# Attention, a 2-D Fourier mix and a split-precision feed-forward on one core: zero products at the start, the second weight's preparation moved later, scale passes tied to finished heads, and a new table of planned times

## The chip, the cores and the metric

The kernel runs on one core of a Trainium2 chip. The metric is the device time of one execution in microseconds (us). The profiled execution is one more run of the same program, recorded by the hardware profiler.

Engines are named as in the profile: PE is TensorE (PEld its weight loads), DVE is VectorE, ACT is ScalarE, POOL is GpSimd, SP is SyncE, whose queue issues nearly all the transfers. Each engine works its own instructions off in order.

## The reference, cut to what matters

```python
# batch B=8, heads H=8, sequence S=576, head size D=64, model width 512, hidden width 2048
scores = q @ k.T / sqrt(D) + slopes[h] * (-abs(i - j))      # only 0 <= i-j < 128, else -1e9
attn   = exp(scores - max); attn /= attn.sum(-1) + 1e-9
x      = (attn @ v)  ->  (B, S, 512)
u      = x + real(fft(fft(x, axis=1), axis=2))
un     = (u - mean(u)) / sqrt(var(u) + 1e-6)
out    = u + relu(un @ w_ch1) @ w_ch2
```

## The kernel before

**Work of a batch.** A batch has four pairs of heads. A pair has scores on PE (`scores`), an exponential with its bias and row minimum on DVE and ACT, a transposition of the probabilities, and products with v (`values`); `weigh` (DVE) divides a finished head into the batch's tile X. After four pairs `fourier` transforms X: `fold_a` to `fold_d` on DVE and ACT, `rows`, `middle` and `cols` as products on PE, evictions on ACT and DVE, sums back into X. `norm` normalizes the rows (DVE, POOL, ACT) and a transposing transfer writes the tile uT. Last comes `ffn`: per tile of 256 rows it has 16 steps of up-products (12 matmuls of 256 columns a step, two steps to a bank) and then, for each 128 rows, 48 down-products of 512 columns. An eviction of hidden values is one ACT instruction (`ACTIVATE hbuf<-fp`, 144 in all) and one of DVE. The up- and down-products share two banks of PSUM (pool `ps_f`).

**Two kinds of pairs.** Batches 0 and 1 (`b < NF`) compute scores and values in 32-bit and transpose on PE (`turn`). Batches 2 to 7 split every operand into two 16-bit parts, and their probabilities are transposed by transfers on SP's queue (`flip`). To split they need a scale of q, k and v of the whole batch. `batch_scales` makes it in a pass: `fetch` brings a 128 by 512 piece of the batch's data into a slot (there are two slots), `part` squares and sums it on ACT, fifteen pieces a batch, six batches, so ninety parts; then `top` and `scale`.

**Weights.** Each of the two weights comes as 64-bit words in sixteen pieces of 512 KB. A piece is loaded, `rebias` (ACT) and `join` (DVE, two instructions) make 32-bit numbers of it, and `gram` (PE, four products) measures it. From the sum of the grams comes a scale, and `high` (ACT) and `low` (DVE) split the weight into two 16-bit planes. `wall_109` holds the first weight, `wall_110` the second.

**Products without use.** After every turn of batches 0 and 1, `warm` multiplies 184 columns into a part of the `pv` bank that nobody reads: `SPIN` times in batch 0, `SPIN1` times in batch 1.

**The order.** Each function is put into a queue with a planned time (`put(t, f)`), and the times come from a table of constants. A scheduler of the framework then sets the order of each engine's instructions from its own estimate of durations, so that an instruction with a later planned time can stand earlier where its inputs are there.

Of the kernel before, what the change touches and what calls it, by code (L numbers as in the profile page):

```python
# [22 lines left out]
NF = 2  # L23
# [17 lines left out]
TGRP = ((0, 1), (2, 3), (4,))  # L41


LB, LC = 2, 5
DFT = 29.33
START = 49.19
PACE, T1 = (0.442, 0.509), 11.5
SPIN, GAP = 6, 1.03
SLOW = 1.318
W2A, W2D, W2B, W2E = 4.44, 0.778, 21.6, 0.559  # L50
W1D, W1B, W1E = 0.507, 13.0, 0.6
F0 = 6.38
SW=184
SPIN1 = 3


def begin_of(p):
# [20 lines left out]
def attn_fft_ffn_kernel(  # L78
# [39 lines left out]
    A.dma_start(out=tab1_sb, in_=tab1)  # L118
    A.dma_start(out=tab2_sb, in_=tab2)
    A.activation(misc[:, 12:13], half[:, 0:1], AF.Exp)  # L120
    stack = const.tile([128, 512], F16, name="stack")
    stack1 = const.tile([128, 1], F16, name="stack1")
    G.memset(stack, 0.0)
    G.memset(stack1, 0.0)
    vhs = const.tile([128, 2, 2, 5, 65], F16, name="vhs")
    G.memset(vhs[:, :, :, :, 64:65].rearrange("p a b c d -> p (a b c) d"), 1.0)
# [2 lines left out]
                    for o in range(0, 4096, 512)])  # L129

    wall = [const.tile([128, 9, 1024], F32, name=f"wall{i}") for i in range(2)]
    mslots = cycle([wall[0][:, 8, o:o + 512] for o in (0, 512)])
    wf = [t.bitcast(F16).rearrange("p s (e x) -> p s e x", e=2) for t in wall]

    def w1_ap(e, c, f):
# [30 lines left out]
    stage = xp.tile([128, 5, DM], F32, name="X").rearrange("p a b -> p (a b)")  # L166

    ready = set()

    def weights(wi, t0, dt, t1, dt1):  # L170
        w, top = ((w1, 2.0 ** 7), (w2, 2.0 ** 14))[wi]
# [54 lines left out]

        for c in range(16):
            t = t0 + dt * c
            put(-3 + 0.1 * c if c < ns else t + dt * (1 - ns) - 0.05, load, c)
            put(t, rebias, c)  # L230
            put(t + dt - 0.1, join, c)
            put(t + 2 * dt - 0.3, gram, c)
# [17 lines left out]
    def batch_scales(b, t0, dt):  # L250
        box = {}

        def begin():
            box["mx"] = small.tile([128, 3, 5], F32, name="mx", tag="mx")
            G.memset(box["mx"], 0.0)

        def fetch(x, fl, o, n):
            assert (0, 7) in ready
            box[x] = next(mslots)[:, 0:n]
            nc.sync.dma_start(out=box[x], in_=fl[:, o:o + n])  # L260

        def part(x, i, c):
            t = box.pop(x)
            A.activation(t, t, AF.Square, accum_out=box["mx"][:, i, c:c + 1])  # L264

        def top():
            m1 = small.tile([128, 3], F32, name="m1")
            V.tensor_reduce(m1, box["mx"], AX.X, ALU.max)
            box["sums"] = total(m1)

        def scale():
            r = small.tile([128, 3], F32, name="r")
            root_inv(r, box["sums"])
            sc = small.tile([128, 8], F32, name="sc", bufs=3)
            V.tensor_scalar_mul(sc[:, 0:1], r[:, 0:1], 2.0 ** -58)
# [12 lines left out]
        put(t0 - 2.5 * dt, begin)  # L288
        x = 0
        for i, (src, n) in enumerate(((q, NQ * 4), (k, NK * 4), (v, 2560))):  # L290
            fl = src[b].rearrange(("j p s -> (j p s)", "h p c d -> (h p c d)")[i == 2])
            fl = fl.rearrange("(p x) -> p x", p=128)
            for c, o in enumerate(range(0, n, 512)):
                put(t0 + dt * (x - 1.8), fetch, x, fl, o, min(512, n - o))
                put(t0 + dt * x, part, x, i, c)
                x += 1
        put(t0 + dt * x, top)
        put(t0 + dt * x + 0.6, scale)

# [37 lines left out]
    def convert(p, what):  # L337
# [8 lines left out]
        if what < 2:  # L346
            pair = att.tile([128, 2, NQ], F16, name="qk"[what] * 2)
            n, s = ((NQ, nsl[:, 8 + j:9 + j]), (NK, sc[:, 1:2]))[what]
            hi, lo, src = pair[:, 0, 0:n], pair[:, 1, 0:n], raws[p][what]
            ops.setdefault(p, []).extend((hi, lo))  # L350
        else:
            s = sc[:, 2:3]
            vh = vhs[:, p % 2]
            vl = att.tile([128, 2, 5, D], F16, name="vl")
            hi = vh[:, :, :, 0:D].rearrange("p a b c -> p (a b) c")
            lo = vl.rearrange("p a b c -> p (a b) c")
            src = raws.pop(p)[2].rearrange("p a b c -> p (a b) c")
            ops[p] += vh, vl
# [100 lines left out]
    def weigh(p, e, pv):  # L459
        b, j = divmod(p, 4)  # L460
        h = 2 * j + e
        if h == 0:
            Xs[b] = xp.tile([128, 5, DM], F32, name="X")
        ri = small.tile([128, 5], F32, name="ri")
# [287 lines left out]
    for p in range(4 * B):  # L752
        b, j = divmod(p, 4)
        t, f = begin_of(p), 1 if b else PACE[0]
        lead = t - 7 * f if p else -3.2
        if p == 4:
            lead = max(lead, begin_of(3) - 3.7 * PACE[0])
        put(lead, load, p)
        if b < NF:
            put(t - 3.8 * f if p else -2, convert, p, 0)  # L760
            put(t - 1.2 * f, load_v, p)
            put(t + 4.2 * f, v_max, p)
        else:
            early = p < 4 * NF + 2
# [9 lines left out]
        if b < NF and j == 3:  # L774
            put(t + 5 * f, f32_scale, b)

    def step(g, t, dt):
        if next(g, g) is not g:
            put(t + dt, step, g, t + dt, dt)

    for b in range(B):
        t = begin_of(4 * b)
        if b >= NF:
            batch_scales(b, *((t - 16.4, 0.72) if b == NF else (t - 26, 1.2)))
        fourier(b, transform_of(b))
# [121 lines left out]
```

## Time and profile before

| | us |
|---|---|
| median of 3 runs (lowest to highest) | 1096.65 (1095.37 to 1097.96) |
| profiled execution | 1097.29 |
| its span, first to last instruction | 1095.5 |
| PE busy | 1047.4 |
| DVE busy | 700.9 |
| ACT busy | 586.0 |

The time of the profiled execution is 1.8 us longer than its span. "Busy" counts modelled ends of pipelined matmuls, so that a busy PE is not one at its peak. A granted clock of 1.00 is 2.4 GHz, of 0.50 is 1.2 GHz.

### The profile page before, as it was taken

To read this page: it belongs to the slowest core of one execution; us is meant where nothing else is said; L and a number is where in the kernel's file an instruction comes from. 1 tells how busy PE (TensorE), PEld (TensorE's weight loads), DVE (VectorE), ACT (ScalarE), POOL (GpSimd) and SP (SyncE) were. 2 spreads that over 40 slices of the span, in tenths; PEclk is the share of its full clock that TensorE was granted. 3 is DMA by queue.
4 is the path that set the end of the run, shared out by engine and by line. 5 is a ranking of instruction groups with operands and counts; after the bars stand their busy time and mean duration, and the time that the engine had idled before them with its cause. 6 is when DMAs were issued, how large, how long until landed. Compare 5 with 4: busy or idle time off the path is not lost.

```text
span 1095.5 us, 23888 instructions
## 1 busy us (share of the span) xinstructions
PE 1047.4 (96%) x9254; PEld 734.7 (67%) x9254; DVE 700.9 (64%) x2073; ACT 586.0 (53%) x1388; POOL 23.8 (2%) x61
## 2 busy tenths in 40 slices
PE   6999989988897999999999999999899999999998
PEld 4886776574655677676757578585758576757655
DVE  4889588558783775959685857777776726252111
ACT  6887888667755674557534745466545512241000
POOL 0000000001000000001000000001000000000000
PEclk9997869999999999999999999999999999999999
DMA  9961475656676364424722454326412410020000
GB/s 370 347 202 55 121 182 160 187 147 145 140 192 182 77 137 88 99 64 73 163 69 69 101 100 87 95 50 124 118 46 46 89 33 10 11 58 11 20 11 20
DMA packets 191506, 117.81 MB, mean 108 GB/s; under 512 B 154400, under 2 KB 164128, under 8 KB 191392
## 3 DMA queue, kind: packets, MB, share of 16 engines
q1 hardware_dynamic: 190816, 114.84, 41.5%
q8 instruction: 72, 1.18, 0.5%
q10 hardware_dynamic: 576, 1.45, 0.3%
q14 instruction: 42, 0.34, 0.1%
HBM read 70.63 MB, written 9.44 MB: 73 GB/s over the span
## 4 chain that ended last, share of the span: by engine, by line
PE 68%; DMA 11%; DVE 8%; ACT 8%; issue 3%; SPq 1%; ACTq 0%; DVEq 0%
PE fp L728 27%; PE fp L743 25%; PE sp L384 5%; PE pv L448 3%; DMA wall<-k_dram 2%; PE pd L579 2%; ACT wall L264 2%; DMA wall<-v_dram 2%; DMA wall<-q_dram 2%; ACT P L163 2%; PE pv L305 1%; DMA pt<-P 1%; DVE P L396 1%; PE pd L613 1%; DMA kr<-k_dram 1%
## 5 line engine op out<-in xcount | busy, mean ns | idle before, releaser
L743 PE MATMUL fp<-wall,hbuf 128*128 128x512 f16 x1728 | 391.2, 380 | 1.9 <-DVE hbuf L163 1.8
L728 PEld LDWEIGHTS <-wall 128*128 128x128 f16 x3840 | 338.1, 98 | 62.9 <-issue 20.0
L728 PE MATMUL fp<-uT,wall 128*128 128x256 f16 x3072 | 365.7, 275 | 14.3 <-DVE hbuf L163 8.5
L743 PEld LDWEIGHTS <-hbuf 128*128 128x128 f16 x1728 | 164.1, 98 | 190.8 <-issue 6.4
L163 ACT ACTIVATE P<-P,nb 128x256 f32<-128x256 f32 x320 | 142.8, 478 | 98.8 <-DVE nb L396 98.3
L733 ACT ACTIVATE hbuf<-fp 128x512 f16<-128x512 f32 x144 | 85.1, 592 | 194.5 <-PE fp L728 194.4
L163 DVE SCALAR_TENSOR_TENSOR hbuf<-fp,hbuf 128x512 f16<-128x512 f32 x144 | 98.3, 683 | 97.5 <-ACT hbuf L733 97.3
L396 DVE CUSTOM_DVE_ANT_0 P<-sp,rg,nsl 128x256 f32<-128x256 f32 x240 | 98.3, 450 | 46.1 <-PE sp L384 38.6
L163 DVE SCALAR_TENSOR_TENSOR P<-P 128x256 f16<-128x256 f32 x240 | 89.0, 391 | 30.5 <-ACT P L409 29.5
L384 PE MATMUL sp<-kk,qq 64*128 64x256 f16 (+4 forms) x880 | 96.1, 296 | 8.3 <-DMA kk<-k_dram 5.5
L409 ACT ACTIVATE P<-P 128x256 f16<-128x256 f32 x240 | 85.3, 383 | 6.6 <-DMA pt<-P 6.1
L264 ACT ACTIVATE wall<-wall 128x512 f32<-128x512 f32 (+2 forms) x90 | 54.5, 606 | 49.5 <-DMA wall<-v_dram 18.4
L453 PE MATMUL pv<-vhs,pt 128*128 128x65 f16 x432 | 54.8, 195 | 4.8 <-DMA pt<-P 3.8
L163 DVE SCALAR_TENSOR_TENSOR X<-fp,misc,X 128x512 f32<-128x512 f32 x32 | 23.9, 746 | 54.1 <-PE fp L743 54.1
L454 PE MATMUL pv<-vl,pt 128*128 128x64 f16 x432 | 54.7, 193 | 0.0
L455 PE MATMUL pv<-vhs,pt 128*128 128x65 f16 x432 | 54.6, 194 | 0.0
L453 PEld LDWEIGHTS <-pt 128*128 128x128 f16 x432 | 40.9, 98 | 14.1 <-DMA pt<-P 4.8
L384 PEld LDWEIGHTS <-qq 64*128 64x128 f16 (+1 forms) x720 | 31.8, 100 | 24.4 <-issue 20.2
L448 PE MATMUL pv<-vr,pt 128*128 128x65 f32 x288 | 46.7, 307 | 0.4 <-issue 0.3
L448 PEld LDWEIGHTS pv<-vr,pt 128*128 128x128 f32 x288 | 43.2, 225 | 3.6 <-issue 1.8
L728 PE MATMUL fp<-wall,wall 128*128 128x128 f16 x768 | 45.0, 219 | 0.0
L454 PEld LDWEIGHTS <-pt 128*128 128x128 f16 x432 | 40.6, 99 | 5.9
(156 smaller groups left out, 1177.5 us busy)
## 6 DMA issues: line engine op xcount, KB each, us to landing
qr<-q_dram SPq DMA_DIRECT2D x32, 304.0 KB, 3.1
hbuf<-w_dram SPq DMA_DIRECT2D x16, 512.0 KB, 7.6
out_dram<-X SPq DMA_DIRECT2D x32, 256.0 KB, 2.4
wall<-v_dram SPq DMA_DIRECT2D x30, 256.0 KB, 2.8
vr<-v_dram SPq DMA_DIRECT2D x24, 320.0 KB, 3.3
kr<-k_dram SPq DMA_DIRECT2D x24, 289.0 KB, 3.3
wall<-q_dram SPq DMA_DIRECT2D x24, 256.0 KB, 2.9
wall<-k_dram SPq DMA_DIRECT2D x24, 256.0 KB, 2.9
```

The source lines that it names most:

```text
L163: put(now[0] + dt, lambda: f(*a, **kw))
L264: A.activation(t, t, AF.Square, accum_out=box["mx"][:, i, c:c + 1])
L384: T.matmul(sp[e][:m, col:col + n], qq[h, c0:c0 + m], keys(kk[h], ti), start=(x == 0), stop=(x == len(prods) - 1))
L396: V.tensor_tensor_reduce(pt[:m, 0:n], sp[e][:m, col:col + n], tab[:m, pc:pc + n], mul, 3.0e38, ALU.add, ALU.min, nb[:m, ti:ti + 1])
L409: A.activation(hi, P32, AF.Copy, scale=2.0 ** 14)
L448: T.matmul(pv[:, ti], pt[:, col:col + 128], ops[p][2][:, e, vc], start=first, stop=last)
L453: T.matmul(pv[:, ti], ph, vh[:, e, vc], start=first, stop=False)
L454: T.matmul(pv[:, ti, 0:D], ph, vl[:, e, vc], start=False, stop=False)
L455: T.matmul(pv[:, ti], pl, vh[:, e, vc], start=False, stop=last)
L728: T.matmul(fp[:, i * n:(i + 1) * n], w1_ap(e, c, f0 + i), uT[:, j, c, 0:n], start=(c == 0 and p == 0), stop=(c == 3 and p == 2))
L733: A.activation(ht[:, 0], fp, AF.Relu)
L743: T.matmul(op, hh[f][:, a, i * 128:(i + 1) * 128], w2_ap(e, f), start=(f == 0 and p == 0), stop=(f == 15 and p == 2))
```

## The change

- **Products from the start.** Twenty matmuls of 512 zero columns (`stack`, now the first tile that POOL fills after `ident`) stand ahead of the first scores and write the bank `pv`; with the bank there, `warm` runs after batch 0's first turn too.
- **Fewer products later.** `SPIN` goes from 6 to 5 and `SPIN1` from 3 to 1. Counted in the order of PE, there are 138 such matmuls in batch 0 before and 120 now, and 72 in batch 1 before and 24 now.
- **Second weight.** Its planned start `W2A` goes from 4.44 to 13.895, its first loads come behind those of the first weight (`WL`).
- **Scale passes.** For batches 3 to 7 a one-element copy on POOL reads the head that `weigh` finished last by plan and writes the slot, and the transfer into the slot waits for the copy: 75 copies. These batches have three slots instead of two.
- **The table.** All planned times are new; `E0` adds a delay once, after the sixteenth step of the feed-forward.

```diff
-LB, LC = 2, 5
-SPIN, GAP = 6, 1.03
-W2A, W2D, W2B, W2E = 4.44, 0.778, 21.6, 0.559
-SPIN1 = 3
+LB, LC = 2, 5.046
+E0 = 18.423
+W1A, N0 = 1.058, 20
+SPIN, GAP = 5, 0.73
+W2A, W2D, W2B, W2E = 13.895, 0.631, 21.285, 0.429
+SPIN1 = 1
...
-    mslots = cycle([wall[0][:, 8, o:o + 512] for o in (0, 512)])
+    mslots = [wall[0][:, 8, 0:512], wall[0][:, 8, 512:1024], wall[1][:, 8, 512:1024]]
+    turns, held = count(), set()
...
-            put(-3 + 0.1 * c if c < ns else t + dt * (1 - ns) - 0.05, load, c)
+            put(WL[wi] + 0.1 * c if c < ns else t + dt * (1 - ns) - 0.05, load, c)
...
         def fetch(x, fl, o, n):
             assert (0, 7) in ready
-            box[x] = next(mslots)[:, 0:n]
-            nc.sync.dma_start(out=box[x], in_=fl[:, o:o + n])
+            slot = next(turns) % (3 if (1, 7) in ready and b > NF else 2)
+            assert slot not in held
+            held.add(slot)
+            box[x] = slot, mslots[slot][:, 0:n]
+            if b > NF:
+                G.tensor_copy(box[x][1][0:1, 0:1], last[-1])
+            nc.sync.dma_start(out=box[x][1], in_=fl[:, o:o + n])
...
-                put(t0 + dt * (x - 1.8), fetch, x, fl, o, min(512, n - o))
+                put(t0 + dt * (x - (FL if b > NF else min(FL, 1.95))), fetch, x, fl, o, min(512, n - o))
...
+    pv = ps_v.tile([128, 512], F32, name="pv")
+    spare_cols["pv"] = pv[:, 512 - SW:512]
+    for _ in range(N0):
+        T.matmul(pv, stack[:, 0:128], stack, start=True, stop=True)
...
+        last.append(Xs[b][0:1, 0, h * D:h * D + 1])
...
     def step(g, t, dt):
         if next(g, g) is not g:
-            put(t + dt, step, g, t + dt, dt)
+            steps[0] += 1
+            t += dt + (E0 if steps[0] == 16 else 0.0)
+            put(t, step, g, t, dt)
```

**ACT during batch 1's transform.** Before, between the evictions of the row products (`zh`, L583) and the first of the middle ones (`gt`, L601), parts of the scale passes (L264, on `wall_109`) stand among them:

```order
L264 ACTIVATE wall_109,mx<-wall_109 128x512 x2
L733 ACTIVATE hbuf<-fp 128x512
L583 ACTIVATE zh_2810<-pd 128x289
L733 ACTIVATE hbuf<-fp 128x512
L359 ACTIVATE vhs<-vr,sc 128x10x64
L264 ACTIVATE wall_109,mx<-wall_109 128x512
L264 ACTIVATE wall_109,mx<-wall_109 128x384
L583 ACTIVATE zh_2847<-pd 128x289
L733 ACTIVATE hbuf<-fp 128x512
L264 ACTIVATE wall_109,mx<-wall_109 128x512 x2
L601 ACTIVATE gt<-pd,sc 128x1 x2
```

Now the same place (`zh` is L606, `gt` L624, evictions of hidden values L757) has none:

```order
L606 ACTIVATE zh_2672<-pd 128x289
L428 ACTIVATE P<-P 96x256
L757 ACTIVATE hbuf<-fp 128x512
L624 ACTIVATE gt<-pd,sc 128x1 x2
L624 ACTIVATE gt<-pd,sc 33x1
L625 ACTIVATE gt<-gt 128x1 x2
L625 ACTIVATE gt<-gt 33x1
L757 ACTIVATE hbuf<-fp 128x512
L644 ACTIVATE ab<-pd,gt,sc 128x65
```

Counted over ACT's whole order, the parts that stand ahead of the 1st, 8th, 16th, 36th, 72nd and 90th of the 144 evictions of hidden values were 19, 27, 56, 90, 90 and 90 before, and are 14, 18, 30, 45, 75 and 90 now.

**PE at the start.** Before, PE begins with the first pair's scores (L384):

```order
L384 MATMUL sp_131<-kk,qq 128x256
L384 MATMUL sp_132<-kk,qq 128x256
L384 MATMUL sp_131<-kk,qq 128x128
L384 MATMUL sp_132<-kk,qq 128x128
L384 MATMUL sp_161<-kk,qq 128x256
```

Now twenty weight loads and products of `stack` (L319) stand ahead of them (L403); the last two are shown:

```order
L319 LDWEIGHTS stack
L319 MATMUL pv<-stack 128x512
L319 LDWEIGHTS stack
L319 MATMUL pv<-stack 128x512
L403 MATMUL sp_149<-kk,qq 128x256
L403 MATMUL sp_150<-kk,qq 128x256
L403 MATMUL sp_149<-kk,qq 128x128
```

The scores have kept their order, behind the new products.

**PE and the second weight's grams.** Before, they (L203 on `wall_110`) stand singly in batch 0's pairs, the first four between the first pair's scores and turns:

```order
L384 MATMUL sp_211<-kk,qq 128x256
L203 LDWEIGHTS wall_110
L203 MATMUL fp<-wall_110 128x128
L203 LDWEIGHTS wall_110
L203 MATMUL fp<-wall_110 128x128
L203 LDWEIGHTS wall_110
L203 MATMUL fp<-wall_110 128x128
L203 LDWEIGHTS wall_110
L203 MATMUL fp<-wall_110 128x128
L384 MATMUL sp_212<-kk,qq 128x256
```

Now all 64 (L211) stand among the row products of batch 0's transform (L602), the first 48 in one piece, of which the beginning is shown:

```order
L446 MATMUL sp_1823<-ident,P 128x128 x2
L602 LDWEIGHTS fh_965
L602 MATMUL fp<-tab_sb,fh_965 128x289
L602 LDWEIGHTS fh_965
L602 MATMUL pd<-tab_sb,fh_965 128x289
L211 LDWEIGHTS wall_110
L211 MATMUL fp<-wall_110 128x128
L211 LDWEIGHTS wall_110
L211 MATMUL fp<-wall_110 128x128
```

So 64 products of 128 columns have moved out of batch 0's pairs into its transform. On DVE sixteen of the second weight's joins stood ahead of batch 0's last `weigh` before, and thirteen do now. Of the 75 copies on POOL, 30 wait in the program for a semaphore of DVE, that is, for a head that was not waited for yet.

## Rows read from the trace of the kernel before

**Rows 1.** Page, part 1: busy us (share of the span) and instructions of an engine.

```profile
PE 1047.4 (96%) x9254; PEld 734.7 (67%) x9254; DVE 700.9 (64%) x2073; ACT 586.0 (53%) x1388; POOL 23.8 (2%) x61
```

**Rows 2.** Windows of the span: length, busy us of each engine, clock, DMA, GB/s.

```profile
0.00:82.00 82.00, 72.34 (x611) 59.52 (x611) 59.75 (x210) 63.04 (x134) 1.52 (x12) 1.00 0.84 307
82.00:150.00 68.00, 61.67 (x393) 49.35 (x393) 48.17 (x161) 52.38 (x130) 2.25 (x7) 0.73 0.39 99
...
175.00:370.00 195.00, 174.26 (x1553) 117.54 (x1551) 132.27 (x391) 132.20 (x352) 3.82 (x11) 0.98 0.64 162
370.00:850.00 480.00, 473.67 (x4533) 326.81 (x4532) 351.74 (x1057) 258.25 (x611) 12.60 (x23) 1.00 0.41 88
...
920.00:1095.50 175.50, 171.72 (x1282) 113.97 (x1280) 48.22 (x91) 31.41 (x64) 2.20 (x6) 1.00 0.08 22
```

**Rows 3.** The same windows for the parts (L264) alone: ACT busy, instructions.

```profile
175.00:370.00 195.00, 45.83 (x132) 0.98 0.64 162
370.00:850.00 480.00, 0.00 (x0) 1.00 0.41 88
```

**Rows 4.** Waits of ACT, 175 to 370 us: total, times, longest.

```profile
ACT wall L264 <- DMA wall<-v_dram: 18.4, 13, 2.4
ACT wall L264 <- DMA wall<-q_dram: 14.9, 10, 4.6
ACT wall L264 <- DMA wall<-k_dram: 12.8, 11, 3.1
```

**Rows 5.** Chain that ended last, 175 to 370 us, shares by line.

```profile
by line: DMA wall<-v_dram 10.4%; DMA wall<-k_dram 9.9%; issue 8.6%; ACT wall L264 8.1%; DMA pt<-P 7.8%; DMA wall<-q_dram 7.6%; PE fp L728 7.1%; ACT P L163 2.7%; SPq L418 2.6%; DVE P L396 2.3%; DVE P L163 2.2%; DMA kr<-k_dram 1.8%; DMA qr<-q
```

**Rows 6.** Waits of PE, 175 to 370 us.

```profile
PE fp L728 <- DVE hbuf L163: 7.5, 10, 1.7
PE pv L453 <- DMA pt<-P: 3.8, 2, 1.9
```

**Rows 7.** Chain, 987 us to the end: start, us, line, instructions.

```profile
1028.96 20.96 PE fp L728 x192
1049.92 20.72 PE fp L743 x96
```

**Rows 8.** Chain, 20.7 to 82 us, shares by line.

```profile
by line: PE pv L448 27.7%; PE sp L384 24.2%; PE pv L305 18.5%; PE sp L427 12.5%; PE fp L203 10.6%; DVE wall L225 1.9%; DVE P L396 1.2%; issue 1.1%; PE pd L148 0.8%; DVE X L470 0.6%; DVE ri L466 0.3%; DVE ri L469 0.3%; DVE nb L396 0.2%; DVE 
```

**Rows 9.** Groups by line, PE, 20.7 to 82 us: count, busy, mean ns, idle before.

```profile
L305 PE MATMUL pv<-pt 128*128 128x184 bf16 x138 | 15.7, 244 | 0.0
...
L203 PE MATMUL fp<-wall 128*128 128x128 bf16 x109 | 10.1, 220 | 0.0
```

**Rows 10.** Windows of all engines, columns as in the second group.

```profile
92.00:106.00 14.00, 12.59 (x53) 9.34 (x54) 13.81 (x42) 10.05 (x20) 0.10 (x1) 0.51 0.20 62
106.00:126.00 20.00, 18.66 (x177) 14.70 (x175) 8.52 (x35) 15.75 (x54) 0.10 (x1) 1.00 0.53 149
126.00:149.00 23.00, 19.96 (x97) 17.72 (x96) 15.31 (x53) 17.40 (x42) 2.04 (x5) 0.51 0.50 105
```

**Rows 11.** Chain, 82 to 150 us, shares by line.

```profile
by line: PE pv L448 17.0%; DMA wall<-k_dram 9.5%; DMA uT<-un 8.0%; PE sp L384 6.9%; PE pv L305 6.7%; ACT wall L264 5.4%; DVE wall L225 5.3%; DVE P L396 5.1%; DMA wall<-q_dram 4.5%; PE sp L427 4.3%; issue 2.3%; DVE fg L515 1.8%; DVE fg L516 
```

**Rows 12.** Timeline of PE, 5 to 30 us: start, us, instructions, idle before.

```profile
5.52 3.36 PE L384 MATMUL sp<-kk,qq 64*128 64x256 f32 x16 [5.52 <-DMA kk<-k_dram]
...
12.11 1.51 PE L427 MATMUL sp<-ident,P 128*128 128x128 f32 x6 [0.66 <-ACT P L163]
...
28.79 0.88 PE L427 MATMUL sp<-ident,P 128*128 128x128 f32 x6
```

**Rows 13.** Timeline of ACT and DVE, 8 to 12 us.

```profile
8.94 0.66 ACT L189 ACTIVATE wall<-hbuf 128x512 f32<-128x512 f32 x1 [4.14 <-DMA hbuf<-w_dram]
...
10.70 0.42 DVE L396 CUSTOM_DVE_ANT_0 P<-sp,rel_sb 128x256 f32<-128x256 f32 x1
```

**Rows 14.** Timeline of POOL at the start.

```profile
0.95 0.53 POOL L123 MEMSET stack<- 128x512 f16 x1
```

**Rows 15.** Waits of SP's queue, 370 to 850 us.

```profile
SPq L418 <- DVE P L163: 166.9, 50, 10.4
```

More of the change, by code (lines that the diff above doesn't have):

```diff
@@ L41 @@
 TGRP = ((0, 1), (2, 3), (4,))
-LB, LC = 2, 5
-DFT = 29.33
-START = 49.19
-PACE, T1 = (0.442, 0.509), 11.5
-SPIN, GAP = 6, 1.03
-SLOW = 1.318
-W2A, W2D, W2B, W2E = 4.44, 0.778, 21.6, 0.559
-W1D, W1B, W1E = 0.507, 13.0, 0.6
-F0 = 6.38
-SW=184
-SPIN1 = 3
+LB, LC = 2, 5.046
+E0 = 18.423
+W1A, N0 = 1.058, 20
+WL = (-2.569, 0.042)
+PL, VL = 8.86, 2.996
+FL, SA, SD, SB, SE = 1.9, 16.181, 0.696, 24.163, 1.152
+DFT = 29.394
+START = 48.432
+PACE, T1 = (0.447, 0.427), 13.742
+SPIN, GAP = 5, 0.73
+SLOW = 1.609
+W2A, W2D, W2B, W2E = 13.895, 0.631, 21.285, 0.429
+W1D, W1B, W1E = 0.379, 11.116, 0.508
+F0 = 6.021
+SW = 184
+SPIN1 = 1
 def begin_of(p):
@@ L113, in attn_fft_ffn_kernel @@
     half, wone, wsc = misc[:, 0:4], misc[:, 6:7], misc[:, 8:11]
+    stack = const.tile([128, 512], F16, name="stack")
+    G.memset(stack, 0.0)
     G.memset(half[:, 0:4], -0.5)
@@ L120, in attn_fft_ffn_kernel @@
     A.activation(misc[:, 12:13], half[:, 0:1], AF.Exp)
-    stack = const.tile([128, 512], F16, name="stack")
     stack1 = const.tile([128, 1], F16, name="stack1")
-    G.memset(stack, 0.0)
     G.memset(stack1, 0.0)
@@ L168, in attn_fft_ffn_kernel @@
     ready = set()
+    weighed, valued = [0] * B, [0] * 4 * B
+    last = []
     def weights(wi, t0, dt, t1, dt1):
@@ L258, in fetch @@
             assert (0, 7) in ready
-            box[x] = next(mslots)[:, 0:n]
-            nc.sync.dma_start(out=box[x], in_=fl[:, o:o + n])
+            slot = next(turns) % (3 if (1, 7) in ready and b > NF else 2)
[5 more added lines that the diff above has]
+            nc.sync.dma_start(out=box[x][1], in_=fl[:, o:o + n])
         def part(x, i, c):
-            t = box.pop(x)
+            slot, t = box.pop(x)
+            held.discard(slot)
             A.activation(t, t, AF.Square, accum_out=box["mx"][:, i, c:c + 1])
@@ L352, in convert @@
             s = sc[:, 2:3]
+            assert p < 2 or valued[p - 2] == 6
             vh = vhs[:, p % 2]
@@ L436, in values @@
         pt = pts.pop((p, i, e))
+        valued[p] += 1
         if i == 0:
@@ L461, in weigh @@
         h = 2 * j + e
+        weighed[b] += 1
         if h == 0:
@@ L503, in begin @@
         def begin():
+            assert weighed[b] == H
             XA = Xs[b]
@@ L677, in norm @@
         else:
+            assert (1, 7) in ready
             uT = wall[1][:, 8, 0:512].bitcast(F16).rearrange("p (e c t) -> p e c t", e=2, c=4)
@@ L754, in attn_fft_ffn_kernel @@
         t, f = begin_of(p), 1 if b else PACE[0]
-        lead = t - 7 * f if p else -3.2
+        lead = t - (7 if b else PL) * f if p else -3.2
         if p == 4:
@@ L760, in attn_fft_ffn_kernel @@
             put(t - 3.8 * f if p else -2, convert, p, 0)
-            put(t - 1.2 * f, load_v, p)
+            put(t - (1.2 if b else VL) * f, load_v, p)
             put(t + 4.2 * f, v_max, p)
@@ L775, in attn_fft_ffn_kernel @@
             put(t + 5 * f, f32_scale, b)
+    steps = [0]
     def step(g, t, dt):
         if next(g, g) is not g:
-            put(t + dt, step, g, t + dt, dt)
+            steps[0] += 1
+            t += dt + (E0 if steps[0] == 16 else 0.0)
+            put(t, step, g, t, dt)
     for b in range(B):
@@ L783, in attn_fft_ffn_kernel @@
         if b >= NF:
-            batch_scales(b, *((t - 16.4, 0.72) if b == NF else (t - 26, 1.2)))
+            batch_scales(b, *((t - SA, SD) if b == NF else (t - SB, SE)))
         fourier(b, transform_of(b))
@@ L787, in attn_fft_ffn_kernel @@
         t = forward_of(b)
-        put(t, step, ffn(b), t, (24 if b else forward_of(1) - t) / n)
-    weights(0, 0.0, W1D, W1B, W1E)
+        put(t, step, ffn(b), t, (24 if b else forward_of(1) - t - E0) / n)
+    weights(0, W1A, W1D, W1B, W1E)
     weights(1, W2A, W2D, W2B, W2E)
```

## The prediction

> **What bounds the kernel now.** The page's busy shares come first: PE 96 %, DVE and ACT far below [rows 1]. That alone would leave a change only PE's own work. The windows by stage say otherwise. From 370 us PE stands idle 6.3 of 480 us, and over the last 175.5 us, a dense run of feed-forward products, 3.8 us; but 9.7 of 82 us at the start, 6.3 of the next 68 at a mean clock of 0.73, and 195 − 174.3 = 20.7 between 175 and 370 us [rows 2]. So early and middle can give time back; the late part can only lose it.
>
> In the middle stretch the parts of the scale passes occupy ACT 45.8 us in 132 instructions, two a part, so 66 parts; later there are none [rows 3]. ACT also waits 46.1 us there for the fetches (18.4 + 14.9 + 12.8) [rows 4], which no other work uses, since ACT goes in order: (45.8 + 46.1) / 66 = 1.39 us of ACT a part, and with its 132.2 us busy ACT is taken for 178 of 195 us [rows 2 to 4]. The chain puts 36 % of the stretch (10.4 + 9.9 + 7.6 + 8.1), 70 us, on these fetches and parts [rows 5]. PE meanwhile waits for few things by name, hidden evictions first (7.5 us) [rows 6]. The end is a PE chain, 0.109 us for an up-product (20.96 / 192) and 0.216 for a down-product of 512 columns (20.72 / 96) [rows 7]. From 20.7 to 82 us the chain is PE at 93 % [rows 8]; from 82 to 150 us it is mixed, with fetches and parts at 19.4 % of 68 us [rows 11].
>
> **The change part by part.** *Unused products.* 18 fewer in batch 0: there they took 18.5 % of 61.3 us of the chain, 11.3 us, and 138 of them is 0.082 us each [rows 8, 9]: −1.5. The 48 fewer in batch 1, two thirds of 6.7 % of 68 us [rows 11]: −3.0, as long as the clock stays as it is (a rival below).
>
> *Second weight's grams.* 10.6 % of 61.3 us over 109 products is 0.060 us each [rows 8, 9], so 64 are 3.8 us. They leave the pairs and come back in batch 0's transform, where the clock is 0.51 [rows 10]: 3.8 at the full, 7.6 at the half clock. In the transform PE waits anyway, so it may cost nothing. Net 0 to +3.8; I take +2. The joins follow the same way on DVE, three fewer ahead of batch 0's last division, which DVE can hide: it has 22 us free in the first 82 [rows 2]. Nothing else needs the second weight before the first down-products; if its planes were late, that would show there as a wait for `wall_110`.
>
> *The first products.* Twenty of 512 columns are 4.3 us at 0.216 each [rows 7], 8.6 at half that speed. `stack` is filled from 0.95 us for 0.53 [rows 14], so they end at 5.8 to 10.1 us; the scores, which now begin at 5.52 when their transfer lands and take 3.36 [rows 12], end by 13.5 instead of 8.9. DVE reads the first scores only at 10.70 and ACT, which waits 4.14 us for the first weight's piece, rebiases at 8.94 [rows 13]: so the loss is at most 2.8 us and may be nothing. The gain: a turn of six takes 1.51 us at 12.11 and 0.88 at 28.79 [rows 12]. If the clock is up for the first pair, four or five such groups and the values between save up to 3. Between −3 and +2.8 I take 0.
> The Trainium skill ("TensorE: Matmul & The Clock Gate", section "What's actually happening") holds that the throttled clock is the default and that activity releases it; that agrees with the two turns [rows 12] and would make this term −2 and the sum 2 us less. By the same rule the cut of `SPIN1` is a danger, which is the first rival.
>
> *Scale passes, early.* Fourteen parts stand ahead of the first hidden eviction instead of nineteen. The chain's 19.4 % of 68 us is 13.2 us [rows 11], 0.7 a part, 3.5 for five; if half of that comes out elsewhere, −2. Bounds −3.5 and 0.
>
> *Scale passes, middle.* This is the main term. Between the 8th and the 36th hidden eviction stand 27 parts (45 less 18) where there were 63 (90 less 27): 36 fewer, 57 %. PE's idle time above the later rate (6.3 / 480 of 195 us is 2.6) is 20.7 − 2.6 = 18.1 us [rows 2]. If all of it comes from ACT's passes, 57 % is 10.4; the third slot lets a fetch start one part earlier and shortens the waits of those that remain, so I take −12. Bounds: 0 (the waits are those of the batches' own transfers) and −18.1.
>
> *Scale passes, late.* 45 parts now come after the 36th eviction, where ACT is busy 258 of 480 us [rows 2]. At the middle's whole idle time a part would cost PE 20.7 / 66 = 0.31 us, so +14 for 45; nothing if they are hidden. Against the upper end: a part with its own wait (1.39 us) can delay a hidden eviction, but two banks alternate, and filling the other one takes PE 24 × 0.109 = 2.6 us [rows 7], more than that hold. Nearer to hidden, then: +4.
>
> *The copies.* 75 on POOL, which works 23.8 us in all [rows 1]; 1.5 of those us in the first 82 [rows 2]. Thirty wait for DVE, and a transfer that waits for them holds SP's queue. SP already waits for DVE 50 times late in the kernel, 167 us in all [rows 15], and PE does not stand for it; the copies read heads that are done about when their batch is reached. I take 0; the price if not is the third rival.
>
> *Sum:* −1.5 − 3.0 + 2 + 0 − 2 − 12 + 4 = −12.5. The profiled execution takes 1097.29, so 1084.8; it lies 0.64 above the median of the runs, so 1084. Transforms and the feed-forward's steps keep their work; `E0` and the rest of the table act through the order, which is counted above.
>
> **The rivals.** *More.* The whole 18.1 us of the middle comes back, the late parts cost nothing, early −7 (grams 0, first products −1): −26, about 1070. For it: ACT was taken for 91 % of the stretch. Against: hidden evictions are only 7.5 us of PE's named waits [rows 6].
>
> *The clock falls in batch 1.* Its stage runs at 0.51, then 1.00 from 106 to 126, then 0.51 [rows 10]; the full clock comes with pairs that hold three unused products a turn. With one, PE could be idle enough to stay at half. The price is at most the stretch's 18.7 busy us times 0.72 (1.51 / 0.88 − 1) [rows 10, 12], +13.4; for half of it +6.7, so 1091, for all 1097, no change. Against: batch 1's real products stay as dense as they were, and the grams' removal changes nothing there.
>
> *A part costs PE the same wherever it stands.* At 0.31 us each, −11.2 for 36 in the middle and +14 late, with −4.5 early: −1.7, 1095. For it: in both stretches the same two banks wait for the same ACT. Against: ACT is half free late.
>
> *The tied transfers hold SP's queue (slower).* The transfer behind a copy waits until the head is divided; behind it on SP stand the transposing transfers of the next head (`flip`), then PE's values. PE's wait for such a transfer was 1.9 us, twice in the middle [rows 6]. From 7 of the 30 copies on (7 × 1.9 = 13.3) the gain is gone; with 13 it is +25, so 1109. For it: SP goes in order, and P already comes late to it (10.4 us at most) [rows 15]. Against: `weigh` follows its values shortly and the feed-forward fills PE while a pair waits.
>
> **How the numbers follow.** Forecast 0.50, more 0.10, clock 0.12, same price 0.12, held queue 0.16. A measurement tells about 0.2 %, 2.2 us, from no change. Faster: the first two, 0.09 of the clock and 0.07 of the same price (with its early terms at their better end), 0.76. Same: the remaining 0.03 and 0.05, 0.08. Slower: 0.16. The forecast's own range is 1072 to 1092 (middle term −18.1 to −6, late 0 to +8, early terms −3 to +3 around the sum, not all at once). The range for 8 in 10 takes in the more, clock and same-price cases and leaves out most of the held queue: 1068 to 1099.
>
> **What the profile will show.** Early: twenty products from about 1.5 us, and turns of six near 0.88 before 20 us; with 1.5 the term is a loss. Clock windows between 90 and 150 us: a stretch at 1.00 during batch 1's pairs, or the first rival with a price is true. First hidden eviction earlier than before in the program by some 5 us. Middle: far fewer than 66 parts between 175 and 370 us, ACT's wait for fetches well under 46 us, PE idle under 12 us, and PE in place of the fetches at the head of the chain. Late: parts of batches 5 to 7 with waits of ACT for fetches, but PE's idle from 370 us on near 1.3 %; if it grows to 3 %, parts cost the same there. SP's waits for POOL: short and few, and no new waits of PE for `pt`. I am wrong if PE's idle time in the middle stays at 20 us with the parts gone (then the batches' own chain, not the passes, made it), or if `pt` waits of 2 us come a dozen times.

## The result and the profile after

The changed kernel takes 1083.1 us (median of four runs, 1081.72 to 1086.17), the kernel before 1097.3 beside it: 0.9869 of it, 95 % interval 0.9833 to 0.9906. The forecast was 1084. That the number came out does not mean that its terms did: two groups of them were off by far and cancelled, so the closeness is luck. The profiled execution took 1086.17, 3 us above the median, so its stages can account for 11.6 us (its span against the one before) and not for all 14.2 between the medians.

First the windows by stage of the kernel after (columns as in [rows 2]):

```profile
0.00:82.00 82.00, 75.95 (x584) 59.16 (x584) 61.03 (x220) 64.65 (x141) 1.52 (x12) 0.96 0.85 307
82.00:150.00 68.00, 60.91 (x474) 49.45 (x473) 53.28 (x164) 55.77 (x132) 2.39 (x10) 0.87 0.43 104
...
175.00:370.00 195.00, 183.34 (x1652) 121.87 (x1651) 138.12 (x423) 112.69 (x283) 13.94 (x35) 0.99 0.50 119
370.00:850.00 480.00, 466.43 (x4421) 321.43 (x4420) 343.46 (x1017) 273.60 (x676) 25.97 (x67) 1.00 0.47 108
```

PE's idle time from 175 to 370 us fell from 20.7 to 195 − 183.3 = 11.7 us. From 370 to 850 us it grew from 6.3 to 13.6. Between 82 and 150 us the mean clock rose from 0.73 to 0.87. The parts (now L278, windows for them alone) stand where the order had put them:

```profile
175.00:370.00 195.00, 17.20 (x50) 0.99 0.50 119
370.00:500.00 130.00, 10.28 (x30) 1.00 0.49 119
500.00:700.00 200.00, 20.63 (x60) 0.99 0.53 126
```

That is 25 parts in the middle (66 before [rows 3]) and 45 behind it. They have taken their waits with them, as the waits of ACT from 370 to 700 us show:

```profile
ACT wall L278 <- DMA wall<-q_dram: 21.7, 10, 5.1
ACT wall L278 <- DMA wall<-k_dram: 19.1, 11, 4.6
ACT wall L278 <- DMA wall<-v_dram: 15.7, 7, 5.2
```

56.5 us for 45 parts, 1.26 each, where it had been 46.1 for 66, 0.70 each [rows 3, 4]. The chain from 175 to 370 us now begins with products, but still holds fetches (9.3 + 4.1 %) and parts (3.3 %), 16.7 % where the two had 36 % in [rows 5]:

```profile
by line: PE fp L752 19.2%; PE fp L767 10.1%; DMA wall<-v_dram 9.3%; issue 5.2%; DMA wall<-q_dram 4.1%; ACT wall L278 3.3%; DVE P L415 3.1%; DVE P L169 3.0%; PE pd L602 2.4%; DVE hbuf L169 2.3%; PE pd L636 2.2%; PE sp L403 2.0%; ACT un L721 
```

**The lead, by equal work.** Idle time in a window says little when the work in it differs. So I cut both executions at the last division of batches 1, 3 and 5 (185.0, 438.7, 674.9 us before; 176.7, 416.9, 663.6 after) and counted feed-forward products in each piece. Before, up-products (L728), then down-products (L743):

```profile
0.00:185.00 185.00, 25.60 (x191) 20.50 (x192) 0.88 0.64 206
185.00:438.70 253.70, 97.30 (x908) 78.31 (x906) 0.99 0.60 146
438.70:674.90 236.20, 102.74 (x963) 83.32 (x962) 1.00 0.42 91
...
0.00:185.00 185.00, 0.00 (x0) 0.00 (x0) 0.88 0.64 206
185.00:438.70 253.70, 99.79 (x432) 41.18 (x432) 0.99 0.60 146
438.70:674.90 236.20, 98.47 (x432) 40.31 (x432) 1.00 0.42 91
```

After (L752 and L767):

```profile
0.00:176.70 176.70, 24.68 (x192) 19.85 (x192) 0.92 0.64 202
176.70:416.90 240.20, 98.91 (x905) 78.72 (x906) 0.99 0.52 123
416.90:663.60 246.70, 104.37 (x963) 84.28 (x961) 0.99 0.49 117
...
0.00:176.70 176.70, 4.55 (x22) 2.18 (x23) 0.92 0.64 202
176.70:416.90 240.20, 94.27 (x412) 38.21 (x410) 0.99 0.52 123
416.90:663.60 246.70, 99.04 (x432) 40.08 (x432) 0.99 0.49 117
```

To batch 1's last division the lead is 185.0 − 176.7 = 8.3 us, and 22 down-products (4.6 us of PE) are done beyond: **12.9 early**. The next piece is 13.5 us shorter, of which those 4.6 were already counted: **8.9 in the middle**. The third holds exactly the same products in 246.7 instead of 236.2 us: **10.5 lost late**. Together −11.3; the spans differ by 11.6. The prediction had −4.5, −12 and +4.

### The profile page after: what moved, and what is told of

The parts are those of the page before. It is cut to its first block, busy times and chain, and to the rows that moved or that the text cites. A ratio compares the mean times of both kernels' runs of the same rounds, so it can differ in the third digit from the quotient of the medians.

```text
span 1083.9 us, 23935 instructions
## 1 busy us (share of the span) xinstructions
PE 1039.0 (96%) x9208; PEld 726.4 (67%) x9208; DVE 703.2 (65%) x2073; ACT 583.0 (54%) x1388; POOL 48.0 (4%) x136
## 4 chain that ended last, share of the span: by engine, by line
PE 61%; DVE 16%; DMA 9%; ACT 7%; issue 3%; SPq 2%; POOL 1%; ACTq 0%; DVEq 0%; POOLq 0%
PE fp L752 25%; PE fp L767 22%; PE sp L403 4%; DMA wall<-v_dram 4%; DVE P L415 2%; DMA wall<-q_dram 2%; ACT wall L278 2%; PE pd L602 2%; PE pv L468 2%; DVE P L169 1%; PE pd L636 1%; DVE hbuf L169 1%; DMA pt<-P 1%; ACT P L169 1%; PE sp L446 1%
## 5 line engine op out<-in xcount | busy, mean ns | idle before, releaser
L767 PE MATMUL fp<-wall,hbuf 128*128 128x512 f16 x1728 | 391.2, 379 | 0.0
L752 PEld LDWEIGHTS <-wall 128*128 128x128 f16 x3840 | 338.5, 99 | 70.4 <-issue 25.2
L752 PE MATMUL fp<-uT,wall 128*128 128x256 f16 x3072 | 365.4, 275 | 20.2 <-DVE hbuf L169 11.9
L767 PEld LDWEIGHTS <-hbuf 128*128 128x128 f16 x1728 | 162.8, 98 | 184.9 <-issue 3.5
L757 ACT ACTIVATE hbuf<-fp 128x512 f16<-128x512 f32 x144 | 84.8, 589 | 202.0 <-PE fp L752 201.9
L169 DVE SCALAR_TENSOR_TENSOR P<-P 128x256 f16<-128x256 f32 x240 | 87.4, 391 | 40.4 <-ACT P L428 38.9
L278 ACT ACTIVATE wall<-wall 128x512 f32<-128x512 f32 (+2 forms) x90 | 54.4, 605 | 91.3 <-DMA wall<-k_dram 33.5
L403 PE MATMUL sp<-kk,qq 64*128 64x256 f16 (+5 forms) x880 | 95.0, 287 | 1.4 <-ACT pt L449 0.7
L403 PEld LDWEIGHTS <-qq 64*128 64x128 f16 (+1 forms) x720 | 32.4, 99 | 24.6 <-issue 18.8
L752 PE MATMUL fp<-wall,wall 128*128 128x128 f16 x768 | 46.2, 219 | 0.0
L468 PEld LDWEIGHTS pv<-vr,pt 128*128 128x128 f32 x288 | 37.6, 199 | 6.1 <-PE pv L323 3.3
L272 POOL COPY wall<-X 1x1 f32<-1x1 f32 x75 | 26.2, 377 | 343.9 <-DVE X L491 265.0
```

Of the source, the lines that this page charges most:

```text
L169: put(now[0] + dt, lambda: f(*a, **kw))
L403: T.matmul(sp[e][:m, col:col + n], qq[h, c0:c0 + m], keys(kk[h], ti), start=(x == 0), stop=(x == len(prods) - 1))
L468: T.matmul(pv[:, ti], pt[:, col:col + 128], ops[p][2][:, e, vc], start=first, stop=last)
L752: T.matmul(fp[:, i * n:(i + 1) * n], w1_ap(e, c, f0 + i), uT[:, j, c, 0:n], start=(c == 0 and p == 0), stop=(c == 3 and p == 2))
L757: A.activation(ht[:, 0], fp, AF.Relu)
L767: T.matmul(op, hh[f][:, a, i * 128:(i + 1) * 128], w2_ap(e, f), start=(f == 0 and p == 0), stop=(f == 15 and p == 2))
```

## The experiments

Three theories at first. *Theory 1* is the prediction's: the crowding of the passes in the middle costs PE, and spread out they are nearly hidden. *Theory 2*: a part costs PE the same wherever it stands, and the gain is made early. *Theory 3*: tied transfers hold SP's queue. Every ratio is to the kernel before, run on the same chip beside it; a difference between two experiments is that of their ratios times 1097.

**E1: the tie alone, in the kernel before.**

```diff
-    mslots = cycle([wall[0][:, 8, o:o + 512] for o in (0, 512)])
+    mslots = [wall[0][:, 8, 0:512], wall[0][:, 8, 512:1024], wall[1][:, 8, 512:1024]]
...
-            box[x] = next(mslots)[:, 0:n]
+            slot = next(turns) % (3 if (1, 7) in ready and b > NF else 2)
+            box[x] = mslots[slot][:, 0:n]
+            if b > NF:
+                G.tensor_copy(box[x][0:1, 0:1], last[-1])
...
+        last.append(Xs[b][0:1, 0, h * D:h * D + 1])
```

> The kernel before with only the fetches of batches 3 to 7 tied to the last finished head and given the third slot; planned times, unused products and the second weight stay as before. In ACT's order 21, 30, 48, 78 and 90 parts then stand ahead of the 8th, 16th, 36th, 72nd and 90th hidden eviction (before 27, 56, 90, 90, 90). Theory 1 (the passes' crowding of the middle stretch costs PE, and spread out they are nearly hidden): the prediction's middle and late terms alone, -12 + 4 = -8, so 0.9927 of the kernel before. Theory 2 (a part costs PE about the same wherever it stands, and the gain of the change is made before 150 us): within 3 us of before, 0.997 to 1.003. Theory 3 (the tied transfers hold SP's queue): slower, over 1.005.

Measured: 1.0068 (1.0039 to 1.0098), slower. The profiled execution, 1114 us, lies above the median of 1103, so its stages are to be read roughly: batch 3's last division came at 424.8 instead of 438.7 us, and then the piece to batch 5's took 261.7 us for nearly the work that took 236.2 (951 up-products instead of 963). The middle gains, the late part loses more. Theory 1 is wrong on the late part. The ratio is the one that theory 3 had named, but its mechanism is not what the trace shows: from 150 to 850 us SP's queue waited 12.4 us for the copies, in 12 waits, and PE waited once for a transposing transfer, 1.6 us. PE's largest wait, for hidden values from DVE, is 20.1 us in all, against 8.5 in the kernel before.

**E2: the changed kernel without the tie.**

```diff
-            if b > NF:
-                G.tensor_copy(box[x][1][0:1, 0:1], last[-1])
```

> The changed kernel without the 75 copies, everything else (table, third slot, first products, second weight) kept. The parts crowd again: 24, 50, 90, 90 and 90 stand ahead of the 8th, 16th, 36th, 72nd and 90th hidden eviction. Theory 1: 8 us are lost, about 1091, 0.994 of the kernel before. Theory 2: no change from the changed kernel, about 0.987. Theory 3: faster than the changed kernel, under 0.984.

Measured: 0.9941 (0.9920 to 0.9962), 7.9 us lost, as theory 1 had it. PE's windows in the crowded stretch, and the late piece's up-products (L750 here):

```profile
250.00:275.00 25.00, 18.57 (x145) 11.47 (x144) 15.91 (x58) 21.39 (x47) 1.59 (x4) 0.86 0.91 212
275.00:300.00 25.00, 15.97 (x163) 12.93 (x164) 24.62 (x65) 19.95 (x53) 0.10 (x1) 0.86 0.93 226
...
434.90:671.60 236.70, 102.89 (x962) 83.13 (x961) 1.00 0.41 91
```

PE is idle 15.5 us in 50, while DMA is busy over 0.9; but the late piece, now without parts, takes 236.7 us again. So the tie is worth more in the middle than it costs late here, and less in E1.

**E3 and E4: one part in five.** The same edit in the kernel before (E3) and in the changed one (E4):

```diff
                 put(t0 + dt * x, part, x, i, c)
-                x += 1
+                x += 1 if b == NF else 5
+                if b > NF:
+                    break
```

> The kernel before with one piece in five in the passes of batches 3 to 7 (15 parts instead of 75), so 60 fetches and parts are left out and the scales of these batches come from a fifth of the data; 57 of the 60 stood between the 8th and the 36th hidden eviction or just ahead. This prices the parts in the middle. Theory 1: PE's 18.1 us of idle time there go, -16 to -18, 0.984. Theory 2: 0.2 to 0.3 us a part, -12 to -18. If the middle's idle time comes from the batches' own chains, -5 or less, over 0.995.

> The changed kernel with the same 60 parts left out of the passes of batches 3 to 7; in it 45 of all 75 stand behind the 36th hidden eviction. This prices them where they now stand. Theory 1: the 45 late ones are nearly hidden (+4 in the prediction), those in the middle a third of before, so -7 us against the changed kernel, about 1076, 0.981. Theory 2: as dear as in the kernel before, 0.2 to 0.3 us each, -12 to -18, 0.971 to 0.976.

Measured: 0.9815 (0.9793 to 0.9837) before, 20.3 us or 0.34 a part; 0.9672 (0.9648 to 0.9696) after, 21.6 us under the changed kernel or 0.36 a part. So the passes cost no less in the changed kernel. Without them the change still gains 0.9815 − 0.9672, 15.7 us: the net gain lies elsewhere, as theory 2 says.

**E5 to E7: parts of the change undone.** E5 `SPIN, SPIN1 = 6, 3`; E6 `N0 = 0`; E7:

```diff
-WL = (-2.569, 0.042)
+WL = (-2.569, -3)
-W2A, W2D, W2B, W2E = 13.895, 0.631, 21.285, 0.429
+W2A, W2D, W2B, W2E = 4.44, 0.778, 21.6, 0.559
```

> The changed kernel with the unused products after a turn as before, 6 in batch 0 and 3 in batch 1 instead of 5 and 1. The prediction's terms turned round: +1.5 and +3.0, so about 1087.6, 0.991 of the kernel before. A rival from the changed kernel's trace: batch 1's stage now lies at a mean clock of 0.87 with one product a turn, and PE waits for others there, so the products cost nothing, 0.987. If the clock gains from more products, faster, under 0.985.

> The changed kernel without the twenty products of 512 columns ahead of the first scores. Prediction: 0, bounds -3 to +3. The trace of the changed kernel shows the first sixteen score products in 1.79 us instead of 3.36, but the first turns at 1.51 us as before; by that the loss without them is at most 1.6 us, 0.987 to 0.9885.

> The changed kernel with the second weight's four planned times and its first loads as before: the grams go back into batch 0's pairs, joins and splits come earlier on DVE and ACT. The prediction has moving it cost 2 us, so by it this kernel is 2 us faster, 0.985. A rival: batch 0's divisions end 6.8 us earlier in the changed kernel because this work left its pairs on DVE and ACT, so 4 to 7 us are lost here, 0.991 to 0.993.

Measured: E5 0.9845 (0.9819 to 0.9871), E6 0.9865 (0.9837 to 0.9893): neither differs from the changed kernel's 0.9869 by more than the intervals. E7 0.9976 (0.9958 to 0.9995): **11.7 us lost**, most of the gain. Windows of E7 around batch 0's transform, then of the changed kernel, where it begins 6.4 us earlier:

```profile
75.00:92.00 17.00, 14.36 (x89) 11.87 (x89) 14.58 (x49) 13.22 (x27) 0.00 (x0) 0.76 0.28 77
92.00:106.00 14.00, 13.00 (x49) 9.01 (x48) 13.88 (x40) 10.14 (x20) 0.10 (x1) 0.50 0.14 44
```

```profile
75.00:92.00 17.00, 13.55 (x70) 9.11 (x71) 16.86 (x55) 15.71 (x31) 0.00 (x0) 0.84 0.25 79
92.00:106.00 14.00, 14.00 (x124) 12.07 (x122) 12.91 (x36) 7.06 (x13) 0.10 (x1) 0.83 0.14 31
```

With the grams back in the pairs, the clock from 92 to 106 us is 0.50, about as in the kernel before [rows 10], and PE does 49 products instead of 124, of which 64 are the grams. The chain of the changed kernel, and two of its windows, show what happens in between:

```profile
92.13 5.01 PE fp L211 x48
...
97.23 0.52 PE fp L211 x9
```

```profile
92.00:96.00 4.00, 4.00 (x40) 4.00 (x39) 3.94 (x12) 2.09 (x5) 0.00 (x0) 0.50 0.00 0
...
97.00:106.00 9.00, 9.00 (x78) 7.08 (x75) 8.03 (x21) 4.44 (x8) 0.00 (x0) 1.00 0.21 48
```

48 grams at 0.104 us, then nine at 0.058: the granted clock rises from 0.50 (1.2 GHz) to 1.00 (2.4 GHz) during them, and what follows up to 106 us, values and turns of batch 1 and the transform, runs at the full clock. That activity releases the throttle is what the Trainium skill ("TensorE: Matmul & The Clock Gate", section "What's actually happening") says, and these rows agree. From 92 to 106 us all the kernels with the new table and the grams in this place (the changed one, E2, E4 to E6, E8, E10 to E12) have 0.83 to 0.98.

Where the loss of E7 lies is seen with both traces cut at the last division of batch 0 (74.7 us, in E7 81.1) and of batch 1 (176.7 and 181.7). First the changed kernel, then E7:

```profile
0.00:74.70 74.70, 69.53 (x542) 54.22 (x542) 53.78 (x197) 57.35 (x126) 1.52 (x12) 0.95 0.90 326
74.70:176.70 102.00, 91.28 (x700) 71.97 (x699) 84.95 (x259) 86.00 (x196) 3.03 (x14) 0.90 0.44 111
...
0.00:81.10 81.10, 73.37 (x604) 58.40 (x606) 58.16 (x206) 61.50 (x132) 1.53 (x12) 0.93 0.81 307
81.10:181.70 100.60, 87.66 (x638) 68.24 (x639) 80.87 (x251) 84.44 (x195) 3.21 (x13) 0.81 0.48 120
```

E7's up- and down-products in the first 181.7 us:

```profile
0.00:181.70 181.70, 24.66 (x192) 19.91 (x192) 0.86 0.63 203
...
0.00:181.70 181.70, 1.26 (x4) 0.44 (x5) 0.86 0.63 203
```

At batch 0's end E7 is 6.4 us behind with the same values and turns done: PE is busy 3.8 us longer, about the grams' time, and idle 2.6 us longer, most of it ahead of the turns, which wait for ACT (the rows of the turns up to these cuts, changed kernel, then E7; the last part is the idle time ahead of them):

```profile
L446 PE MATMUL sp<-ident,P 128*128 128x128 f32 (+1 forms) x86 | 14.4, 296 | 0.9 <-ACT P L169 0.9
L446 PE MATMUL sp<-ident,P 128*128 128x128 f32 (+1 forms) x86 | 14.6, 289 | 3.3 <-ACT P L169 2.4 <-ACT pt L449 0.9
```

At batch 1's end it is 5.0 us behind with 18 down-products (3.9 us) fewer, 8.9 in all. So 6.4 of the 8.9 come from the pairs that the work left, and 2.5 from the stage that took it, which in the changed kernel holds 64 grams and 18 down-products more and is only 1.4 us longer, at a mean clock of 0.90 instead of 0.81. In the next piece E7 falls 3.6 us further behind, with 10.0 us of waits of PE for `pt` from 175 to 370 us, and in the third it is 2.7 us faster.

**E8: transfers left out.**

```diff
-            nc.sync.dma_start(out=box[x][1], in_=fl[:, o:o + n])
+            if b == NF or x < 3:
+                nc.sync.dma_start(out=box[x][1], in_=fl[:, o:o + n])
```

> The changed kernel with only the first three transfers of each pass of batches 3 to 7; the other 60 are left out, their copies on POOL and all 75 parts on ACT stay (the parts square whatever lies in the slot, so the scales of these batches are not those of the data). It divides the price of a part, 0.38 us by the run with 60 parts left out (22.6 us under the changed kernel), into ACT's own work and the wait for the transfer. ACT waits 87.3 us for fetches from 175 us on and works 48 us. If the wait is what PE pays, about two thirds of the 22.6, -14, 1069, 0.974. If it is ACT's work, -3 or less, 0.984 or more.

Measured: 0.9698 (0.9674 to 0.9723), 18.8 us under the changed kernel, 87 % of E4's 21.6. The parts' own 0.7 us on ACT is nearly free (2.8 us for 60 of them, within the intervals); the transfers are what PE pays for, either because ACT stands waiting for them (its waits for fetches and copies from 175 to 850 us fell from 87.3 to 38.9 us) or because of their traffic. The late piece took 239.3 us for the same products, 7.4 of the 10.5 lost ones back. Before, after and in E8:

```profile
438.70:674.90 236.20, 233.91 (x2251) 161.56 (x2250) 173.71 (x525) 126.86 (x298) 6.00 (x11) 1.00 0.42 91
416.90:663.60 246.70, 238.58 (x2251) 163.52 (x2249) 175.12 (x526) 144.94 (x359) 16.57 (x42) 0.99 0.49 117
406.90:646.20 239.30, 236.56 (x2251) 162.97 (x2250) 174.44 (x526) 145.34 (x358) 19.36 (x42) 1.00 0.42 97
```

PE's idle time there is 2.3, 8.1 and 2.7 us; the rest of the loss is that the same 2251 products keep PE busy longer.

**E9: the second weight alone, in the kernel before.**

```diff
-W2A, W2D, W2B, W2E = 4.44, 0.778, 21.6, 0.559
+W2A, W2D, W2B, W2E = 13.895, 0.631, 21.285, 0.429
...
-            put(-3 + 0.1 * c if c < ns else t + dt * (1 - ns) - 0.05, load, c)
+            put((-3, 0.042)[wi] + 0.1 * c if c < ns else t + dt * (1 - ns) - 0.05, load, c)
```

> The kernel before with only the second weight moved: its four planned times and its first loads as in the changed kernel, all else as before. All 64 grams then stand in batch 0's transform. If moving it is the main gain of the change (12.7 us were lost where it was undone in the changed kernel), -8 to -13, 0.988 to 0.993. If that loss came only from other constants of the new table that expect the late weight, 0.997 to 1.003. By the prediction's term, +2, 1.002.

Measured: 1.0117 (1.0094 to 1.0140), 12.8 us *slower*, against all three expectations. The first hidden eviction did end earlier, at 150.0 instead of 157.1 us. But by batch 1's last division, now at 210.4 instead of 185.0 us, PE had done 220 up- and 96 down-products instead of 191 and none (windows for L728, then L743, with the next piece behind):

```profile
0.00:210.40 210.40, 28.16 (x220) 22.66 (x221) 0.88 0.62 198
210.40:460.10 249.70, 97.99 (x878) 78.77 (x876) 0.93 0.55 134
...
0.00:210.40 210.40, 21.22 (x96) 9.35 (x96) 0.88 0.62 198
210.40:460.10 249.70, 76.81 (x336) 31.41 (x336) 0.93 0.55 134
```

At 0.109 and 0.216 us [rows 7] the 29 and 96 products more are 23.9 us of the 25.4, so by equal work nothing had been gained by then. The next piece is 4.0 us shorter than before, with 30 and 96 products (24.0 us) less in it: 20.0 us are lost there. The feed-forward of batch 0 had been put ahead of batch 1's pairs, so batch 1's transform came late, and then PE ran dry. The window, and the wait of PE that fills most of it:

```profile
275.00:300.00 25.00, 5.44 (x85) 4.52 (x82) 18.67 (x58) 17.48 (x47) 2.55 (x6) 0.64 0.60 156
```

```profile
PE fp L728 <- DMA uT<-un: 16.3, 1, 16.3
```

One wait of 16.3 us for the tile of batch 1 that the next up-products read. So the second weight's move gains early in the new table alone, and in the old one it lets the feed-forward run ahead of batch 1 and then run dry. The clock tells the same; windows of E9 from 75 to 106 us:

```profile
75.00:92.00 17.00, 16.35 (x76) 12.40 (x76) 14.32 (x46) 11.13 (x23) 0.00 (x0) 0.67 0.19 59
92.00:106.00 14.00, 13.52 (x104) 10.59 (x102) 12.53 (x40) 10.12 (x18) 0.10 (x1) 0.67 0.15 45
```

In the kernel before these are 1.00 and 0.51: with the grams in the transform the clock is higher from 92 us on, but it had fallen sooner.

**E10 to E12: an attempt at a faster version.** In the changed kernel copies wait up to 18.5 us for a head. E10 reads `last[-2]`, E11 also sets `FL` to 2.8, E12 also takes the old counts 6 and 3.

> The changed kernel with the copies reading the head before the last finished one. In the changed kernel copies wait up to 18 us for the division of a head, and the parts behind stand up to 5 us on ACT for the transfer. If that wait is what the transfers cost PE (18 us by the run without them), half of it comes back here, -5 to -10 against the changed kernel, 1073 to 1078, 0.978 to 0.982. If parts wait for the transfers' own 3 us, no change, 0.986 to 0.988. If earlier fetches crowd forward, slower, over 0.989.

> As the run with the tie one head back, and the transfers planned 2.8 parts ahead instead of 1.9. Each part is 1.152 units of the plan apart and a batch of 24 units takes some 115 us, so this is 5 us earlier, longer than the longest wait for a transfer late in the kernel. If the wait is what PE pays, -8 to -14 against the changed kernel, 1069 to 1075, 0.974 to 0.980; if not, 0.986 to 0.988.

> As the run before, with 6 and 3 unused products a turn as in the kernel before. Those alone gave 0.9845 instead of 0.9869, inside both intervals. If real, another -2.4, 0.972 to 0.978; by the prediction's terms +4.5, 0.978 to 0.984.

Measured: 0.9896 (0.9872 to 0.9920), 0.9903 (0.9881 to 0.9925) and 0.9963 (0.9944 to 0.9981). None is faster than the changed kernel, the last is slower: in E11's order the old counts 6 and 3 cost 6.6 us, where in the changed kernel (E5) they had no measurable cost. ACT's waits for fetches from 175 to 850 us fell only from 87.3 to 73.2 us (E10) and 28.0 + 27.3 + 16.8 = 72.1 (E11), so an earlier issue did not bring the data ahead of the part; and PE's idle time from 370 to 850 us was 15.2 and 20.5 us instead of 13.6.

## Why the prediction was right, and where it was not

The time was within 1 us of the forecast by terms that were wrong in opposite directions: early −12.9 against −4.5, late +10.5 against +4. That the number came so close is luck.

- **The second weight, +2: the step that failed.** By equal work in the profiled executions it gains 8.9 us up to batch 1's last division (E7), the largest term. The leaving half was priced at the grams alone, 3.8 us; the pairs of batch 0 end 6.4 us later in E7, 3.8 of PE's work and 2.6 of its idle time. The prediction put the weight's other work in the pairs at nothing, and spoke of the joins on DVE alone; the idle time is ahead of turns that wait for ACT (3.3 us against 0.9), for which the sum has no term. E7 puts grams, joins and splits back at once, and their shares were not separated. The coming half was priced as a cost, 3.8 to 7.6 us at the clock of the transform, as if the clock were given; it came out as a gain of 2.5, and the clock rose among the grams. I had priced what the products take, not what their place does to the clock. That the clock makes the 2.5 is the likely reading and not shown, since the joins and splits moved too.
- **The rest of the early gain, 4.0 us,** is in no run by itself: E5 and E6 find nothing in the unused and the first products, and what the five parts fewer ahead of the first hidden eviction (−2) and the other new times of the table give was not tried.
- **Passes, late, +4: mis-sized, 10.5.** Of the two bounds I stayed near the wrong one. That two banks would cover a part's hold did not come true: the same products took 10.5 us more with 30 parts among them, 0.35 a part, and E2's piece without parts took 236.7. The price I had set as the upper bound (0.31) was about the price. By which wait PE pays it is open: its waits for hidden values are 3.1 us in this piece. E8 puts most of it on the transfers. E4's piece with six parts still took 241.9 us, so it is not strictly per part.
- **Passes, middle, −12: right in direction, 8.9 by equal work**, and PE's idle time there 11.7 us, as "under 12" had it. E2 shows that the tie makes it: without it PE stood idle 25.3 of these 195 us. Middle and late together are +1.6 us where the prediction had −8, so against the kernel before the spread as such gained nothing.
- **Unused products, −1.5 and −3.0: not found in this order.** E5 has them back at no measurable cost; E12 against E11 has them cost 6.6 us, so their price hangs on the order around them. The chain's share in batch 1's stage may have counted time in which PE would have waited for something else; that was not shown.
- **The first products, 0: right.** They ran from 1.46 us, and the sixteen scores behind them took 1.79 us instead of 3.36 at a granted clock of 1.00, as the timeline of PE shows. But at the first turns the clock was 0.50, and they were as slow as before (columns as in [rows 12]):

```profile
1.46 6.09 PE L319 MATMUL pv<-stack 128*128 128x512 f16 x20 [1.46 <-POOL misc L122]
7.48 1.79 PE L403 MATMUL sp<-kk,qq 64*128 64x256 f32 x16
...
12.32 1.51 PE L446 MATMUL sp<-ident,P 128*128 128x128 f32 x6 [0.86 <-ACT P L169]
```

  In the kernel before the clock column reads 1.00 over these first microseconds too [rows 2], though its turns take the same 1.51 us there; it reads 1.00 also over the slow beginning of the twenty products (ten in 3.5 us, the other ten in 2.5). At the start of a trace the durations are to be believed, not that column.

- **The rivals.** *Same price* had the mechanism right (E3, E4: 0.34 and 0.36 a part) and its time wrong, since its early sum was mine. *Held queue* is refuted in the changed kernel: from 370 to 700 us SP waited 5.9 us for the copies, and PE once for `pt`, 1.1 us, as these rows of SP and PE show (it is PE's only such wait in the whole execution):

```profile
SPq L273 <- POOL wall L272: 5.9, 8, 2.3
...
PE pv L473 <- DMA pt<-P: 1.1, 1, 1.1
```

  In E7, with the same copies in another order, PE waits 11.5 us for `pt` in four waits, and SP 15.5 us for the copies from 150 to 850 us; whether the one makes the other was not tried. *The clock falls* is refuted too: it rose from 0.73 to 0.87 between 82 and 150 us.

What stays open: why parts cost more with the tie in the old table (E1) than in the new; whether ACT's wait or the traffic is what PE pays for the transfers; what the other new times of the table do, `E0` among them, since no run sets them back alone; and what the new table does without the tie and the second weight's move together, which was not tried.

## What to carry to other kernels

A piece of work that is moved has a price where it leaves and another where it arrives, and the second depends on that place: grams priced as a cost in a stage at half clock went with a higher clock there and a small gain, and the stage that they left gained more than their own time. Parts of one change need not add up: the tie and the second weight's move each made the old kernel slower (7.5 and 12.8 us), and they are worth 7.9 and 11.7 us in the new one. For the second weight the trace shows why the old table loses: the dense work ran out before the next batch's tile was ready. For the tie it is open. To find where a lead is won and lost, cut both executions at the same piece of work and count what else was done by then.

## What the runs showed of the hardware that was not expected

More unused products did not mean a higher clock. With 6 and 3 of them a turn (E12) the stretch from 126 to 150 us ran at 0.64, with 5 and 1 (E11) at 0.86; the kernels differ in these counts alone, though the order moves with them. It is one execution of each, and E5 against the changed kernel is mixed: 0.78 against 0.85 from 126 to 149 us, but 0.92 against 0.83 from 92 to 106. E12's window, then E11's:

```profile
126.00:150.00 24.00, 23.61 (x145) 20.55 (x144) 16.13 (x51) 20.73 (x44) 3.18 (x10) 0.64 0.64 157
```

```profile
126.00:150.00 24.00, 21.38 (x168) 18.60 (x168) 16.95 (x51) 21.10 (x40) 2.63 (x8) 0.86 0.65 148
```

PE looks busier at the lower clock (23.61 against 21.38 us) and does fewer products (145 against 168): busy time at a lower clock is not work done.
